# A first weight load moved to another queue and ahead of the other loads, with its conversion two items earlier in the program

## The chip, the cores and the metric

The kernel runs on one core of one Trainium2 chip. The metric is the device time of one execution in microseconds (us), lower is better. The engines are named as the profile names them: PE (TensorE matmul), PEld (its weight load), DVE (VectorE), ACT (ScalarE), POOL (GpSimd) and SP (SyncE, which only issues transfers). "SPq" and "ACTq" are the sequencers of SP and ACT at the moment they issue a transfer.

## What is computed

Three layers follow each other on 3072 tokens (4 batches of 768) of width 512. First comes attention with 8 heads of width 64, in which each query sees 8 global keys and the 96 latest keys, with a distance bias per head. Then a gated layer with float64 weights, and then a "soft" mixture of experts with 32 slots. Cut to what matters:

```
scores = q @ k.T / 8 + bias(head, distance)      # kept where global or local
x  = softmax(scores) @ v                         # 3072 x 512
h  = x @ w_in                                    # w_in 512 x 2048, float64
g  = h * sigmoid(h)
x2 = g @ w_out                                   # w_out 2048 x 512, float64
logits = x2 @ phi                                # 32 slots
slots  = softmax(logits, over tokens).T @ x2
out    = softmax(logits, over slots) @ experts(slots)   # 8 experts: relu(s @ w1) @ w2
```

## The kernel before

**Tiles and stages.** Attention works on 24 tiles `T` of 128 queries, the gated layer on 8 chunks of 3 tiles. Products in the gated layer are made of f16 halves (a high and a low part of each operand), three matmuls for one product. Attention of the first three tiles (T = 0, 1, 2) comes first, alone; after that the matmuls of a chunk are the main line and the attention of the next chunk's tiles is woven in between them.

**Attention of one tile.** `s_step(T, pr)` makes the scores of one pair of heads: two or four matmuls (L316) into the two score banks, on DVE a bias-add with a row minimum for each head (L331, with a small read of the accumulator after it), on ACT the exponential (L332). After two pairs (half a tile) the probabilities are split into a high part (L200 on ACT) and a low part (L208 on DVE) and turned by a transfer (L349, `DMA_TRANSPOSE`, issued by SP). `pv_step` multiplies the turned halves by v (L371). The two score banks are shared by successive pairs, so the matmuls of the next pair start when DVE has read the last one. `load(T)` issues four transfers on SP: q, the two halves of k, and v. `split(T)` makes the two halves of v (L200, L210).

**Float64 weights.** `w_in` and `w_out` arrive as 16 parts of 1024 KB of 64-bit words (L451). `conv(p)` turns part `p` into the two f16 halves with six larger operations that follow each other across the engines: L461 on ACT (takes a byte of each word), L463 on DVE, two short matmuls L468 on PE (a check of bits that must be zero, with the small matrix `wz`), L471 on DVE, then L481 on ACT (high half) and L489 on DVE (low half). `w_ahead()` issues the loads of the next parts whose place is free; parts 1 to 6 are also held back until a given half of an attention tile is done (`GATE`, by a one-column write on POOL, L356). The first matmuls of the gated layer are L503 to L505.

**The prologue** (L779 on) loads the two counts `n_global` and `n_local` and three distance tables (`shapes`, 192 KB) on ACT's queue, and on SP's queue tile 0, the identity matrix (`ident`, 64 KB of `shapes`), tile 1, weight part 0, tile 2 and `phi`. DVE makes the distances from the counts and tables (L794 to L806), then `wz` from `ident` (L811, L812); POOL makes `ident16` from `ident` and then the bias tables of the later tiles (L818); ACT makes the bias table of tile 0 (L814).

**What sets the order.** Program order is written by hand: `first_items()` lists the steps of the first three tiles, and `START` says after which item each of the first parts is converted:

```
START = [3, 9, 14, 18, 22, 99, 99, 99]
...
        for i, it in enumerate(first_items()):
            it()
            while nconv < 8 and before[nconv] <= i:
                conv(nconv)
```

Items 0, 1, 3 and 4 are the four pairs of heads of tile 0, item 2 is the split of tile 1, item 5 its first product with v. From this program a scheduler lays down, at build time, a fixed list for each engine, in which independent steps may change places. Every engine then works through its list in order, and a step that has to wait holds what stands behind it. Transfers use eight counters in turn (`DMAHW0` to `DMAHW7` in the lists), given out in program order: a transfer is not issued before the earlier one on its counter has landed.

Of the kernel before, what the change touches and what calls it, by code (L numbers as in the profile page):

```python
# [10 lines left out]
I32 = mybir.dt.int32  # L11
# [68 lines left out]
        return self.view(self.take(n), dims, dtype)  # L80


START = [3, 9, 14, 18, 22, 99, 99, 99]
AHEAD = [0, 0, 0, 0, 0, 5, 8, 11, 13, 15]
HE = 'AAAAAAAA'
PHE = 'AAAAAAA'
# [14 lines left out]
def fast_kernel(tc, keepp, q_l, k_l, v_l, q_f, k_f, n_global, n_local, w_in, w_out, phi, w1, w2, shapes, pick_c, out):  # L101


    nc = tc.nc
# [5 lines left out]
    with ExitStack() as ctx:  # L110
# [4 lines left out]
        ar = Arena(pool.tile([128, NB // 4], F32, name="arena"), NB)  # L115
# [137 lines left out]
        def paired(T):  # L253

            return T < NPAIR

        def q_of(T):
            return q32[2 if T == 2 else T % 2]

        def load(T, bufs):  # L260
            if paired(T):
                nc.sync.dma_start(out=q_of(T), in_=q_f[T])
                for z in range(2):
                    nc.sync.dma_start(out=kr32[:, z, 0:4, T % NR], in_=k_f[T][:, :, 64 * z:64 * z + 64])
                nc.sync.dma_start(out=v_at[T], in_=v_l[T])
                return
            for s, src in zip(bufs, (q_l, k_l, v_l)):
                nc.sync.dma_start(out=s, in_=src[T])
            staged[T] = bufs
# [26 lines left out]
        def s_step(T, pr):  # L296
# [41 lines left out]
            if lp == 1:  # L338
                pb, ptb = p16[half], pt[half].rearrange("p z h s c -> p (z h s) c")
                if t == 0:  # L340
                    pb = pb.rearrange("p z h c -> p (z h c)")[:, 0:1024].rearrange("p (z h c) -> p z h c", z=2, h=4)
                if T < C0 and PTE[2 * T + half] != "D":
                    n = w // 32
                    flip(ptb[:, 0:n], ptb[:, n:2 * n], pfb.rearrange("p h c -> p (h c)"), PTE[2 * T + half])
                    held = ptb[:, 2 * n - 1, 127:128]
                else:
                    hi(PHE[T] if T < len(PHE) else CFG["phi"], pb[:, 0, :, :w], pfb[:, :, :w], 0)
                    lo(PLE[T] if T < len(PLE) else CFG["plo"], pb[:, 1, :, :w], pfb[:, :, :w], 0, pb[:, 0, :, :w])
                    nc.sync.dma_start_transpose(out=ptb[:, 0:w // 16], in_=pb.rearrange("p z h c -> p (z h c)"))  # L349
                    held = pb[:, 1, 3, w - 1:w]  # L350
                if T < C0:
                    done_p.add((T, half))
                    p = nload[0]
                    if p < 16 and GATE.get(p) == (T, half) and holder.get(place[p]) is None:

                        G.tensor_scalar(out=ar.view(place[p], [16], F32)[:, 0:1], in0=held, scalar1=1.0, scalar2=0.0, op0=ALU.mult, op1=ALU.add)  # L356
                    w_ahead()
# [38 lines left out]
        def first_items():  # L396
            items = []
            for T in range(C0):
                items.append(lambda T=T: s_step(T, 0))
                items.append(lambda T=T: s_step(T, 1))  # L400
                if T:
                    items.append(lambda T=T: pv_step(T - 1, 1))
                if T + 1 < C0:
                    items.append(lambda T=T: split(T + 1))
                else:
                    items.append(lambda T=T: load(C0, stage_m))
                items.append(lambda T=T: s_step(T, 2))
                items.append(lambda T=T: s_step(T, 3))
                items.append(lambda T=T: pv_step(T, 0))
            items.append(lambda: pv_step(C0 - 1, 1))  # L410
            items.append(lambda: split(C0))
            items.append(lambda: load(C0 + 1, stage_m))
            return items
# [27 lines left out]
        place = [wq[0], wq[1], wq[2], wq[3], we[0], we[1], wq[0], wq[1], we[0], wq[2], wq[3], we[1], we[0], wq[3], we[1], we[0]]  # L441
# [2 lines left out]

        done_p = set()

        def w_ahead():
            while nload[0] < most[0] and holder.get(place[nload[0]]) is None and (GATE.get(nload[0]) is None or GATE[nload[0]] in done_p):
                p = nload[0]
                holder[place[p]] = p  # L450
                nc.sync.dma_start(out=ar.view(place[p], [2048], I32), in_=(w_in if p < 8 else w_out)[p % 8].bitcast(I32))  # L451
                nload[0] += 1

        def conv(p):
# [33 lines left out]
            else:  # L488
                V.scalar_tensor_tensor(out=dst[1], in0=src, scalar=-p2(e - 128), in1=dst[0], op0=ALU.mult, op1=ALU.subtract)  # L489
            holder[place[p]] = None  # L490
            w_ahead()


# [286 lines left out]
        for i, src in enumerate((n_global, n_local)):  # L780
            nc.scalar.dma_start(out=cw[:, 2 * i:2 * i + 2], in_=src.bitcast(I32).rearrange("(o n) -> o n", o=1).to_broadcast([128, 2]))
        nc.scalar.dma_start(out=rel.rearrange("p s c -> p (s c)"), in_=shapes[:, 0:384])
        load(0, None)
        nc.sync.dma_start(out=ident, in_=shapes[:, 384:])
        for T in range(1, C0):
            load(T, None)
            if T == 1:
                w_ahead()
        ph = ar.view(g0 + 20480, [4, NS], F32)
        nc.sync.dma_start(out=ph, in_=phi)  # L790
        hi("P", ident16, ident, 0)
# [30 lines left out]
        nconv = 0  # L822
        before = START
        for i, it in enumerate(first_items()):
# [563 lines left out]
```

## Time and profile before

| | |
|---|---|
| time, median of 3 runs | 716.47 us (713.61 to 717.72) |
| the profiled execution's own time | 718.77 us |
| its span, first to last instruction | 717.0 us |
| busy share of the span: PE, DVE, ACT, POOL | 93%, 69%, 51%, 34% |
| mean granted TensorE clock | 0.987 |
| DMA | 120.08 MB, mean 167 GB/s |

The busy shares are means over stages with different limits: the opening with attention alone, the first chunk with the conversion of the weights beside it, a long middle, and the expert layer at the end. So the stages are read one by one, by the busy time of each engine in stretches of the span, and inside the opening by the instructions in order of time and by what ended each wait. A row of the timeline gives start, duration, engine, line, operation, what it writes and reads, how many are merged in it, and in brackets the idle time of its engine just before it with what ended it. DMA shares are means over the core's 16 DMA engines and can pass 1 where transfers overlap in an engine.

### The profile page before, as it was taken

What the parts mean: (1) busy time and instruction counts of PE and PEld (TensorE: products, weight loads), DVE (VectorE), ACT (ScalarE), POOL (GpSimd) and SP (SyncE); (2) the same over time, 40 slices, a digit from 0 to 9 for tenths busy, and PEclk for the clock granted to TensorE, in tenths of its full rate; (3) what the DMA queues carried; (4) which work ended last, traced back from release to release, by engine and by line L of the source; (5) the groups of instructions that cost most, each with busy time, mean ns of one, the idle gap of its engine ahead of it and who ended that gap; (6) DMA issues with size and microseconds to landing.
All of it is one profiled execution on the core that took longest, in us unless ns stands there. A gap on an engine that the chain in (4) does not pass through costs nothing.

```text
span 717.0 us, 13665 instructions
## 1 busy us (share of the span) xinstructions
PE 669.4 (93%) x5175; PEld 387.1 (54%) x5175; DVE 497.6 (69%) x1191; ACT 363.2 (51%) x910; POOL 240.6 (34%) x201
## 2 busy tenths in 40 slices
PE   4779988899999999999999999999999989999992
PEld 2445543356655664566556655665566546665552
DVE  4999889988754876487638763876386159797432
ACT  5678876556523552356235522652265157574322
POOL 3110002125543556254625572346143400280000
PEclk9999999999999999999999999999999999999997
DMA  7999847783572558426734665355433892296998
GB/s 223 236 293 264 263 135 162 221 191 82 114 149 74 114 123 194 93 49 119 163 77 107 141 161 97 81 118 114 65 46 62 224 302 78 80 370 239 388 400 289
DMA packets 165257, 120.08 MB, mean 167 GB/s; under 512 B 143936, under 2 KB 150464, under 8 KB 159168
## 3 DMA queue, kind: packets, MB, share of 16 engines
q1 hardware_dynamic: 163968, 118.15, 62.9%
q10 hardware_dynamic: 1216, 0.99, 0.4%
q8 instruction: 42, 0.69, 0.4%
q14 instruction: 31, 0.25, 0.1%
HBM read 79.01 MB, written 6.29 MB: 119 GB/s over the span
## 4 chain that ended last, share of the span: by engine, by line


## 5 line engine op out<-in xcount | busy, mean ns | idle before, releaser
L202 POOL TENSOR_SCALAR arena<-arena 128x1024 f16<-128x1024 f32 (+4 forms) x107 | 110.2, 1040 | 299.9 <-ACT arena L332 100.5
L503 PE MATMUL bank<-rows,arena 128*128 128x384 f16 x512 | 168.2, 329 | 0.3 <-ACT rows L200 0.3
L504 PE MATMUL bank<-rows,arena 128*128 128x384 f16 x512 | 168.1, 328 | 0.0
L505 PE MATMUL bank<-rows,arena 128*128 128x384 f16 x512 | 168.0, 328 | 0.0
L200 ACT ACTIVATE arena<-bank 128x384 f16<-128x384 f32 (+1 forms) x153 | 77.3, 505 | 149.9 <-DVE bank L509 85.8
L332 ACT ACTIVATE arena<-arena 128x256 f32<-128x256 f32 (+1 forms) x192 | 92.4, 482 | 84.8 <-DVE arena L331 83.6
L524 PE MATMUL bank<-arena 128*128 128x512 f16 x336 | 127.7, 380 | 1.1 <-DVE arena L489 1.0
L525 PE MATMUL bank<-arena 128*128 128x512 f16 x336 | 127.6, 380 | 0.0
L523 PE MATMUL bank<-arena 128*128 128x512 f16 x336 | 126.6, 381 | 0.7 <-ACT arena L481 0.7
L210 DVE SCALAR_TENSOR_TENSOR arena<-bank,arena 128x384 f16<-128x384 f32 (+2 forms) x154 | 87.7, 570 | 29.5 <-ACT arena L200 28.7
L208 POOL TENSOR_TENSOR arena<-arena 128x1024 f16<-128x1024 f32 (+1 forms) x43 | 89.4, 2080 | 25.4 <-ACT arena L200 22.5
L331 DVE CUSTOM_DVE_ANT_0 arena<-bank,arena 128x256 f32<-128x256 f32 (+1 forms) x192 | 70.2, 394 | 30.9 <-PE bank L326 27.7
L509 DVE SCALAR_TENSOR_TENSOR bank<-arena,bank 128x384 f32<-128x384 f32 x128 | 71.2, 558 | 29.2 <-ACT arena L507 28.2
L208 DVE TENSOR_TENSOR arena<-arena 128x1024 f16<-128x1024 f32 (+2 forms) x52 | 69.4, 1334 | 9.9 <-POOL arena L202 8.8
L200 ACT ACTIVATE arena<-arena 128x1024 f16<-128x1024 f32 (+1 forms) x69 | 62.0, 904 | 19.6 <-DVE arena L210 8.4
L210 DVE SCALAR_TENSOR_TENSOR arena<-arena 128x1024 f16<-128x1024 f32 (+3 forms) x64 | 64.2, 1017 | 7.3 <-POOL arena L202 4.2
L505 PEld LDWEIGHTS <-arena 128*128 128x128 f16 x512 | 50.4, 98 | 33.8 <-issue 1.0
L503 PEld LDWEIGHTS <-arena 128*128 128x128 f16 x512 | 50.5, 99 | 33.2 <-issue 5.0
L507 ACT ACTIVATE arena<-bank 128x384 f32<-128x384 f32 x128 | 61.6, 481 | 12.3 <-PE bank L505 11.5
L504 PEld LDWEIGHTS <-arena 128*128 128x128 f16 x512 | 50.4, 98 | 28.3 <-issue 1.0
L525 PEld LDWEIGHTS <-arena 128*128 128x128 f16 x336 | 33.0, 98 | 41.9 <-issue 3.6
L523 PEld LDWEIGHTS <-arena 128*128 128x128 f16 x336 | 32.8, 98 | 36.2 <-issue 2.6
(185 smaller groups left out, 814.5 us busy)
## 6 DMA issues: line engine op xcount, KB each, us to landing
arena<-in_w_dram SPq DMA_DIRECT2D x31, 1024.0 KB, 8.5
arena<-in_q_l_dram SPq DMA_DIRECT2D x18, 512.0 KB, 3.7
arena<-in_k_l_dram SPq DMA_DIRECT2D x18, 512.0 KB, 4.3
arena<-in_w_in_dram SPq DMA_DIRECT2D x8, 1024.0 KB, 6.0
arena<-in_w_out_dram SPq DMA_DIRECT2D x8, 1024.0 KB, 6.0
arena<-in_v_l_dram SPq DMA_DIRECT2D x24, 256.0 KB, 3.3
out_dram<-arena SPq DMA_DIRECT2D x4, 768.0 KB, 8.6
arena<-in_q_f_dram SPq DMA_DIRECT2D x6, 256.0 KB, 5.2
```

The costliest lines, as they stand in the source:

```text
L200: A.activation(out=out, in_=in_, func=AF.Copy, scale=p2(e))
L202: G.tensor_scalar(out=out, in0=in_, scalar1=p2(e), scalar2=0.0, op0=ALU.mult, op1=ALU.add)
L208: (V if eng == "V" else G).tensor_tensor(out=out, in0=in_, in1=h, op=ALU.subtract)
L210: return V.scalar_tensor_tensor(out=out, in0=in_, scalar=p2(e), in1=h, op0=ALU.mult, op1=ALU.subtract)
L332: A.activation(out=pw, in_=pw, func=AF.Exp, scale=-1.0, bias=nmx[:, T, h:h + 1], accum_out=psum_[T % 2][:, h:h + 1])
L503: mm(hp, wh, x[:, 0, k], start=(k == 0), stop=False)
L504: mm(hp, wh, x[:, 1, k], start=False, stop=False)
L505: mm(hp, wl, x[:, 0, k], start=False, stop=(k == 3))
L509: gated.append(V.scalar_tensor_tensor(out=hp, in0=th, scalar=1.0, in1=hp, op0=ALU.add, op1=ALU.mult))
L523: mm(op, gh, woh[:, f, 0], start=(f == 0), stop=False)
L524: mm(op, gh, woh[:, f, 1], start=False, stop=False)
L525: mm(op, gl, woh[:, f, 0], start=False, stop=(f == 15))
```

## The change

Weight part 0 is no longer loaded by SP after tile 1, but by ACT's queue, right behind the tables and ahead of everything that SP loads in program order; and its conversion is written after item 1 instead of after item 3.

```diff
-START = [3, 9, 14, 18, 22, 99, 99, 99]
+START = [1, 9, 14, 18, 22, 99, 99, 99]
...
-        def w_ahead():
+        def w_ahead(queue=nc.sync):
...
-                nc.sync.dma_start(out=ar.view(place[p], [2048], I32), in_=(w_in if p < 8 else w_out)[p % 8].bitcast(I32))
+                queue.dma_start(out=ar.view(place[p], [2048], I32), in_=(w_in if p < 8 else w_out)[p % 8].bitcast(I32))
...
         nc.scalar.dma_start(out=rel.rearrange("p s c -> p (s c)"), in_=shapes[:, 0:384])
+        w_ahead(nc.scalar)
         load(0, None)
         nc.sync.dma_start(out=ident, in_=shapes[:, 384:])
         for T in range(1, C0):
             load(T, None)
-            if T == 1:
-                w_ahead()
```

The lists of the engines change from the start to about the 300th row of DVE's list, and not behind that. Three places follow. The first is ACT's list, from the load of the tables on (L814 is L813 in the changed file). Before:

```order
L782 DMA arena<-in_shapes_dram 128x384
L814 ACT_TABLE_LOAD
L814 ACTIVATE arena<-arena 128x128 x8
L200 ACTIVATE arena<-arena 128x8x64
L332 ACTIVATE arena<-arena 128x128 x4
L200 ACTIVATE arena<-arena 128x8x64
L200 ACTIVATE arena<-arena 128x512
L332 ACTIVATE arena<-arena 128x128 x3
L461 ACTIVATE arena<-arena 128x1024
```

And with the change:

```order
L782 DMA arena<-in_shapes_dram 128x384
L451 DMA arena<-in_w_in_dram 128x2048
L813 ACT_TABLE_LOAD
L813 ACTIVATE arena<-arena 128x128 x8
L200 ACTIVATE arena<-arena 128x8x64
L332 ACTIVATE arena<-arena 128x128 x4
L461 ACTIVATE arena<-arena 128x1024
L200 ACTIVATE arena<-arena 128x512
L200 ACTIVATE arena<-arena 128x8x64
```

The load of part 0 stands ahead of the table load, and the first step of its conversion (L461) ahead of the split of tile 0's first half (L200, 128x512), where it stood behind that split and behind seven of tile 0's eight exponentials (L332).

The second is DVE's list at the end of tile 0's scores (128x128; tile 1's are 128x256). Before:

```order
L331 ISA arena<-bank_70,arena 128x256
L331 ISA arena 128x1
L463 TENSOR_SCALAR arena<-arena 128x1024
L331 ISA arena<-bank_71,arena 128x256
L331 ISA arena 128x1
L382 TENSOR_SCALAR arena<-arena 128x8
L471 SCALAR_TENSOR_TENSOR arena<-arena 128x1024
L208 TENSOR_TENSOR arena<-arena 128x512
```

And with the change:

```order
L331 ISA arena<-bank_71,arena 128x128
L331 ISA arena 128x1
L463 TENSOR_SCALAR arena<-arena 128x1024
L208 TENSOR_TENSOR arena<-arena 128x512
L471 SCALAR_TENSOR_TENSOR arena<-arena 128x1024
L210 SCALAR_TENSOR_TENSOR arena<-arena 128x4x32
L210 SCALAR_TENSOR_TENSOR arena<-arena 128x8x64
L331 ISA arena<-bank_70,arena 128x256
```

L463 and L471 have moved from between and behind the second pair of tile 1 to straight behind tile 0's last pair; the L208 that the first turning transfer waits for now stands behind L463.

The third is SP's list, with what each transfer waits for, from the load of `ident` on. Before:

```order
L784 DMA arena<-in_shapes_dram 128x128
L262 DMA arena<-in_q_f_dram 128x512 [waits DMAHW0_49]
L264 DMA arena<-in_k_f_dram 128x4x64 [waits DMAHW1_49]
L264 DMA arena<-in_k_f_dram 128x4x64 [waits DMAHW2_49]
L265 DMA arena<-in_v_l_dram 128x512 [waits DMAHW3_49]
L451 DMA arena<-in_w_in_dram 128x2048 [waits DMAHW4_49]
L262 DMA arena<-in_q_f_dram 128x512 [waits DMAHW5_49]
```

And with the change, from the load of `ident` and then from the load of `phi`:

```order
L785 DMA arena<-in_shapes_dram 128x128 [waits DMAHW0_49]
L262 DMA arena<-in_q_f_dram 128x512 [waits DMAHW1_49]
L264 DMA arena<-in_k_f_dram 128x4x64 [waits DMAHW2_49]
...
L789 DMA arena<-in_phi_dram 128x128 [waits DMAHW1_49]
L264 DMA arena<-in_k_f_dram 128x4x64 [waits DMAHW2_49]
L264 DMA arena<-in_k_f_dram 128x4x64 [waits DMAHW3_49]
L265 DMA arena<-in_v_l_dram 128x512 [waits DMAHW4_49]
L349 DMA_TRANSPOSE arena<-arena 128x8x128 [waits DMAHW5_49,DVE_49,Pool_49]
```

Part 0 has taken a counter, so all later transfers are one counter further on: `ident` now waits for counter 0, which `n_global` uses. And the loads of k and v of tile 3 stand ahead of the first turning transfer; before, they stood some ten places behind it.

## Rows read from the trace of the kernel before

**Rows 1.** Busy time by stage: us, then each engine's busy time, clock, DMA

```profile
9.40:52.60 43.20, 31.92 (x198) 19.32 (x198) 38.72 (x95) 33.35 (x81) 9.14 (x17) 1.00 0.96 260
52.60:170.00 117.40, 108.61 (x728) 56.81 (x728) 106.41 (x212) 83.49 (x187) 15.33 (x12) 0.97 0.74 198
170.00:570.00 400.00, 399.06 (x3143) 235.31 (x3142) 259.65 (x695) 175.34 (x522) 189.60 (x142) 1.00 0.53 110
```

**Rows 2.** What DVE waited for in 9 to 53 us: total, times, longest

```profile
DVE arena L331 <- PE bank L316: 2.0, 3, 1.1
DVE arena L208 <- ACT arena L200: 0.8, 2, 0.5
DVE arena L331 <- ACT arena L332: 0.8, 1, 0.8
DVE arena L471 <- PE bank L468: 0.6, 2, 0.4
```

**Rows 3.** Timeline of the first 10 us: start, duration, engine, instruction

```profile
1.65 0.45 ACTq L782 DMA_DIRECT2D arena<-in_shapes_dram  x1
...
3.24 0.43 SPq L784 DMA_DIRECT2D arena<-in_shapes_dram  x1
4.36 0.33 SPq L262 DMA_DIRECT2D arena<-in_q_f_dram  x1
...
7.04 0.43 SPq L451 DMA_DIRECT2D arena<-in_w_in_dram  x1
...
8.13 0.30 POOL L202 TENSOR_SCALAR arena<-arena 128x128 f16<-128x128 f32 x1 [1.18 <-DMA arena<-in_shapes_dram]
...
8.82 0.33 DVE L811 SCALAR_TENSOR_TENSOR arena<-arena 128x32 f32<-128x32 f32 x2
...
9.49 0.28 DVE L331 CUSTOM_DVE_ANT_0 arena<-bank,arena 128x128 f32<-128x128 f32 x1
```

**Rows 4.** Transfers issued before 20 us: queue, count, KB each, median us to landing

```profile
arena<-in_shapes_dram SPq DMA_DIRECT2D x1, 64.0 KB, 4.8
```

**Rows 5.** Busy time by stretch, columns as in rows 1; last two: DMA share, GB/s

```profile
0.00:6.00 6.00, 0.00 (x0) 0.00 (x0) 0.48 (x5) 1.28 (x1) 0.82 (x9) 1.00 0.40 110
6.00:9.00 3.00, 0.80 (x4) 0.54 (x4) 2.18 (x11) 0.40 (x2) 0.53 (x3) 1.00 1.17 319
9.00:12.50 3.50, 2.08 (x9) 1.50 (x9) 1.90 (x16) 3.50 (x17) 3.36 (x7) 1.00 1.04 391
```

**Rows 6.** DMA queues in 4.5 to 6 us: packets, MB, share (q1 SP's, q10 ACT's)

```profile
q1 hardware_dynamic: 712, 0.19, 54.7%
q10 hardware_dynamic: 209, 0.20, 37.3%
```

**Rows 7.** Timeline of 12 to 21 us, part 0's conversion and tile 1's scores

```profile
12.27 1.13 ACT L200 ACTIVATE arena<-arena 128x512 f16<-128x512 f32 x2
...
15.37 1.36 SPq L349 DMA_TRANSPOSE arena<-arena  x1
...
17.31 0.42 DVE L331 CUSTOM_DVE_ANT_0 arena<-bank,arena 128x256 f32<-128x256 f32 x1 [1.07 <-PE bank L316]
...
17.66 1.30 DVE L463 TENSOR_SCALAR arena<-arena 128x1024 uint16<-128x1024 uint16 x1
...
19.67 1.23 DVE L471 SCALAR_TENSOR_TENSOR arena<-arena 128x1024 int32<-128x1024 int32 x1 [0.38 <-PE bank L468]
...
20.71 0.82 PE L371 MATMUL bank<-arena 128*128 128x64 f16 x12
```

**Rows 8.** DVE's groups in 9.4 to 24.8 us: count | busy us, mean ns

```profile
L210 DVE SCALAR_TENSOR_TENSOR arena<-arena 128x512 f16<-128x512 f32 x3 | 2.1, 687 | 0.0
...
L208 DVE TENSOR_TENSOR arena<-arena 128x512 f16<-128x512 f32 x2 | 1.4, 678 | 0.0
...
L489 DVE SCALAR_TENSOR_TENSOR arena<-arena 128x1024 f16<-128x1024 f32 x1 | 1.2, 1221 | 0.0
```

**Rows 9.** What ACT waited for in 10 to 60 us

```profile
ACT arena L461 <- DMA arena<-in_w_in_dram: 4.0, 2, 2.6
```

## The prediction

> **What bounds the kernel now.** I read the busy time by stage first, because one mean over the span hides where a gain can count. From 170 to 570 us PE is busy 399.06 of 400 us [rows 1]: there nothing can be won or lost by loads and conversions, and whatever the opening gains or loses is handed on unchanged to the end. In the opening it is another engine: from the first score step to the first matmul of the gated layer (9.4 to 52.6 us) DVE is busy 38.72 of 43.2 us and PE only 31.92 [rows 1]. So the question is what the change does to DVE's list up to about 52 us. The work on it is the same; only its waits can change. What DVE waited for in that stretch is 2.0 + 0.8 + 0.8 + 0.6 = 4.2 us in all [rows 2], and that is the most that any filling of gaps can bring there, 0.6% of the time. The third view is the timeline of the first 21 us with the transfers [rows 3 to 7], to see which of these waits the change touches and which new one it can make.
>
> **The change part by part.** Sums are made against the profiled execution, 718.77 us (span 717.0 and 1.77 around it); the median of the runs is 716.47, 2.3 lower, and the forecast is put on the median.
>
> *Issue on ACT, one transfer fewer on SP.* An issue on ACT's sequencer takes 0.45 us [rows 3]. It delays the load of ACT's table, but ACT's work of the first 6 us is that load alone, 1.28 us [rows 5], and 0.45 more still ends inside them; its next work waits for DVE's tables: cost nothing. SP's 0.43 us at 7.04 [rows 3] goes; SP's next loads then wait for counters or for full DMA engines: gain nothing.
>
> *Where the megabyte moves.* Part 0 was issued at 7.04 [rows 3]; it will be issued near 2.1, behind the tables (issue at 1.65, 0.45 long). It does not start at once: ACT's queue is still moving the tables in 4.5 to 6 us, 209 packets and 0.20 MB, next to SP's queue [rows 6]. So I expect its bytes from about 6 us on, not in the idle DMA time before (share 0.40 over the first 6 us, rows 5). From 6 us to past 12 the DMA engines are full, share 1.17 and 1.04 [rows 5], so what part 0 gains there, SP's loads lose. The rate of a stretch with its 1.05 MB in it is 391 GB/s [rows 5]: 2.7 us of all engines. Alone, part 0 would be through at 8.7, at half speed at 11.4; ACT's L461 comes to it behind the first four exponentials, in the place where two L200 start at 12.27 now [rows 7]: no wait taken.
>
> *Who loses: `ident`.* DVE's L811 needs `ident`, and stands in front of the first L331. Before, `ident` was issued at 3.24 and landed 4.8 us later [rows 3, 4], at 8.04: POOL started on it at 8.13 and DVE at 8.82 [rows 3], 0.8 us to spare. Now two things push it. Its issue waits for counter 0, that is for `n_global` to land; the q load that waited for that counter before was issued at 4.36 [rows 3], so that is 1.1 us later than 3.24. And its bytes, behind tile 0's v in SP's queue, share the engines with part 0. Lower end: SP's queue is behind anyway, the later issue costs nothing and small packets pass: landing 8.04, no delay. Upper end: all of part 0 first and the later issue in full: 8.04 + 2.7 + 1.1 = 11.84, 3.0 us after 8.82. In 4.5 to 6 us the two queues shared the engines, 54.7% to 37.3% [rows 6], neither shut out; with such a sharing about half of part 0's 2.7 us falls before `ident`, 1.3, and of the 1.1 about half: landing near 9.9, and the first L331 moves from 9.49 to about 10.5. **+1.0 us** (0 to +3.0). POOL's `ident16` moves as much, and its bias tables with it; they are used by tile 1 only, and tile 1's first L331 moves back too: nothing.
>
> The Trainium skill's page "DMA: Bandwidth & Descriptors", section "Queues, rings and completion order", says that each DMA engine goes round its queues packet by packet; rows 6 agree that neither queue is shut out. By that rule part 0 gets every second turn against all of SP's loads, and as its rows (8 KB for each partition) are longer than theirs (2 KB and less), most of the time until it is through; the start term would lie near +2 and the sum at +0.9.
>
> *Conversion sooner.* L463 runs at 17.66 now, between two pairs of tile 1, and L471 at 19.67 behind a wait of 0.38 for PE's L468 [rows 7]. The L331 before L463 waited 1.07 us for the scores of tile 1's second pair [rows 7], since nothing else stood between two pairs that share the score banks. With the change L463, L208, L471 and two L210 come before tile 1's first pair, and L489 and L208 between its first and second: 1.2 + 0.7 us of work [rows 8] where DVE waited 1.07. That wait goes: **-1.1 us**. The wait for L468 stays, because only one L208 (0.7 us, rows 8) stands between L463 and L471: 0. Bounds: 0, if the wait only moves to tile 1's third pair, and -2.0, if all three waits of L331 for PE go [rows 2].
>
> *First turning transfer later.* L208 of tile 0's first half now stands behind L463 (1.30 us) but ahead of one L210 (0.7, rows 8): 0.6 us later, with the start 1.6. The transfer went out at 15.37 and its first user, L371, ran at 20.71 [rows 7], landing to use over 2 us: covered, 0. Without that cover it would cost up to 1.6 on PE, not on DVE.
>
> *Tile 3's k and v before it.* These 512 KB move at 391 GB/s [rows 5] in 1.3 us. SP issues them when tile 1's loads have landed, which PE needs before tile 1's scores and so before the L208 in question: no hold for the turning transfer, whose cover of 2 us takes in the 1.3 too. Later they are missing from the stretch in which L461 waited 4.0 us for its loads [rows 9], a wait of ACT and not of DVE. 0 (-1.3, if such a wait reaches DVE, to +1.3, if they hold the first turning transfer beyond its cover).
>
> *The new order up to 165 us.* Same instructions, other neighbours. From 52.6 to 170 us DVE is idle 11.0 us and PE 8.8 [rows 1]; I have no row that says which way these go. 0, bounds 2 us either way.
>
> **Sum:** +1.0 - 1.1 + 0 = -0.1 us, so 718.7 for the profiled execution and **716.4 us** on the median. A measurement of this kernel tells some 0.5% from no change, 3.6 us; the forecast is no measurable change, between 714 and 719.
>
> **Rivals.**
> *Slower: `ident` behind the megabyte.* The upper end above: DVE stands at L811 until 11.84, +3.0, and as tile 1's loads come as late, the wait of 1.07 is not filled but moves; with the 0.38 in front of L471 doubled the sum is +3.4, 719.9. It decides at a landing of 8.82 us: each us beyond is one of DVE. For it: full DMA engines and the 0.8 us to spare. Against it: the two queues shared in rows 6, and SP's queue is busy with v in any case. The round-robin rule of the Trainium skill cited above speaks for it. Chance 0.16, about half of it past 0.5%.
> *Faster: gaps closed everywhere.* Part 0 is converted while tile 0's data are still on the way, `ident` is not late, and with L463 to L489 out of tile 1 and the early loads of tile 3 the rest of the list meets ready data: the 4.2 us of rows 2 go, 712.3. For it: the loads for which L461 waited 4.0 us [rows 9]. Against it: in the new list L463 comes only after tile 0's last L331, so the waits before 14 us stay. Chance 0.20.
> *Not what it says.* If ACT's queue is served last, part 0 comes behind all that moves from 6 to 12.5 us: 3.0 x 1.17 + 3.5 x 1.04 = 7.2 us of full engines [rows 5], until 13.2. Then `ident` is on time, but L461 holds ACT, and through it L463 holds DVE, by 13.2 - 12.3 = 0.9 us. The start term is as large as before, and the case lies inside the forecast.
>
> **How the numbers follow.** Forecast 0.64, slower rival 0.16, faster rival 0.20. Faster by over 0.5%: 0.15 of the faster rival and 0.04 of the forecast's order term, 0.19. Slower by over 0.5%: 0.07 of the slower rival and 0.05, 0.12. Within: 0.69. The range reaches to both rivals' times, 712.6 to 720.0, and leaves out about 0.2.
>
> **What would show it.** In the changed profile: the first packets of ACT's queue beyond the tables near 6 us; L811 at 9 to 11 us and the first L331 0.7 after it; L463 near 15 us with no L331 waiting 1.07 for PE behind it; the first L503 within 1.5 us of 52.6; PE as full from 170 to 570 us. The prediction is wrong if L811 waits past 11.8, if L463 waits for the load, if L371 begins to wait over 2 us for the turning transfers, or if the stretch from 52.6 to 170 us changes its length by more than 2 us.

## The result and the profile after

The changed kernel takes 722.06 us (median of 6 runs, 719.53 to 725.01), the kernel before on the same chip 715.64 us (6 runs): ratio 1.0092, 95% interval 1.0062 to 1.0121. Run once more among the experiments, it took 722.81 us against 716.95, ratio 1.0083 [1.0057, 1.0108]. The change costs about 6 us, nearly twice the 0.5% that a measurement of this kernel can tell, and the time lies beyond both ranges that the prediction gives (714 to 719, and 712.6 to 720.0 further down). The profiled execution of the change took 725.01 us (span 723.2), 6.2 more than that of the kernel before, so the two traces show a difference of the measured size.

Two places make it up. The first is the start. The first timeline rows answer to [rows 3]; the load of `ident` is L785 here and L784 there, and behind that loop line numbers are one lower than before (L810 here is L811 there). Timeline of the change, first 13 us:

```profile
2.13 0.47 ACTq L451 DMA_DIRECT2D arena<-in_w_in_dram  x1
...
4.43 0.33 SPq L785 DMA_DIRECT2D arena<-in_shapes_dram  x1
...
10.99 0.80 PE L316 MATMUL bank<-arena 64*128 64x128 f32 x4 [10.99 <-DMA arena<-in_k_f_dram]
...
11.79 0.44 DVE L810 SCALAR_TENSOR_TENSOR arena<-arena 128x32 f32<-128x32 f32 x2 [2.01 <-DMA arena<-in_shapes_dram]
11.84 0.33 POOL L202 TENSOR_SCALAR arena<-arena 128x128 f16<-128x128 f32 x1 [3.80 <-DMA arena<-in_shapes_dram]
...
12.71 0.28 DVE L331 CUSTOM_DVE_ANT_0 arena<-bank,arena 128x128 f32<-128x128 f32 x1
```

Part 0 goes out on ACT's queue at 2.13. `ident` goes out at 4.43 instead of 3.24 and DVE stands 2.01 us at L810 for it, until 11.79 instead of 8.82 [rows 3]. The first L331 starts at 12.71 instead of 9.49: 3.2 us lost. Its landing, in the view of transfers issued in 4.5 to 6 us (as [rows 4]):

```profile
arena<-in_shapes_dram SPq DMA_DIRECT2D x1, 64.0 KB, 7.3
```

7.3 us instead of 4.8. The queues show why. In 7 to 9 us of the change (q1 is SP's queue, q10 ACT's: packets, MB, share of the 16 engines):

```profile
q10 hardware_dynamic: 98, 0.77, 94.2%
q1 hardware_dynamic: 137, 0.05, 9.4%
```

and in the same 2 us of the kernel before:

```profile
q1 hardware_dynamic: 1269, 0.62, 117.2%
```

SP's queue, with all of the tiles' loads on it, falls from 1269 packets to 137 while part 0 moves. Neither queue is shut out by count (137 packets to 98), but a packet of part 0 is 0.77 MB / 98 = 7.9 KB and one of SP's 0.4 KB, so SP gets 6% of the bytes. Being first in did not help either: tile 0's k was issued at 1.21 us, ahead of part 0 at 2.13, and PE's first L316 waited for it until 10.99.

The second place is at 158 to 168 us. Three rows of the change, one an engine, from their timelines:

```profile
161.60 1.62 POOL L202 TENSOR_SCALAR arena<-arena 128x1024 f16<-128x1024 f32 x2 [14.51 <-DMA arena<-in_k_l_dram]
...
162.67 1.62 DVE L208 TENSOR_TENSOR arena<-arena 128x1024 f16<-128x1024 f32 x1 [3.20 <-POOL arena L202]
...
167.84 0.38 PE L545 MATMUL bank<-arena 128*128 128x64 f16 x8 [2.79 <-DVE arena L548]
```

Read from the top: POOL waits for a k load, DVE 3.20 us for POOL, PE 2.79 us for DVE. In the kernel before this is PE's longest wait from 145 to 170 us:

```profile
PE bank L524 <- DVE arena L489: 0.3, 1, 0.3
```

The load is tile 9's k, and SP's queue tells why it is late. Timeline of SP's queue of the change (L536 is the turning transfer of chunk 0's second product):

```profile
150.67 0.33 SPq L268 DMA_DIRECT2D arena<-in_q_l_dram  x1
152.00 1.24 SPq L536 DMA_TRANSPOSE arena<-arena  x1
153.28 1.32 SPq L349 DMA_TRANSPOSE arena<-arena  x1
154.69 2.98 SPq L536 DMA_TRANSPOSE arena<-arena  x2
157.72 0.57 SPq L268 DMA_DIRECT2D arena<-in_k_l_dram  x1
```

and of the kernel before:

```profile
145.34 0.33 SPq L268 DMA_DIRECT2D arena<-in_k_l_dram  x1
147.07 0.33 SPq L268 DMA_DIRECT2D arena<-in_v_l_dram  x1
149.12 2.62 SPq L536 DMA_TRANSPOSE arena<-arena  x2
```

DVE's L208 on tile 8's k, which frees the place that tile 9's k is loaded into, before and in the change:

```profile
144.10 1.21 DVE L208 TENSOR_TENSOR arena<-arena 128x1024 f16<-128x1024 f32 x1
```

```profile
152.08 1.22 DVE L208 TENSOR_TENSOR arena<-arena 128x1024 f16<-128x1024 f32 x1
```

Before, k goes out at 145.34, when that L208 is done. In the change DVE takes tile 7's first scores first, that L208 comes at 152.08, and three L536 stand ahead of k on SP: 157.72, 12.4 us later. Of these, 8.0 us are the later end of L208 (153.30 instead of 145.31), and the other 4.4 the transfers that still stand ahead of k then. Nothing of this touches the line that was edited; it is the new order of lists, 150 us downstream.

The stages, answering to [rows 1] (us, then busy time of PE, PEld, DVE, ACT, POOL, clock, DMA share, GB/s):

```profile
9.40:52.60 43.20, 31.08 (x164) 17.94 (x165) 35.09 (x90) 31.83 (x81) 9.23 (x18) 1.00 0.97 251
52.60:170.00 117.40, 106.80 (x721) 55.54 (x719) 107.71 (x210) 81.41 (x177) 14.49 (x11) 0.97 0.70 196
170.00:570.00 400.00, 399.29 (x3147) 236.04 (x3145) 262.43 (x701) 178.29 (x532) 188.27 (x141) 1.00 0.53 109
```

PE is as full from 170 us on as before, so what the opening lost is handed on: the tanh of block 28 runs at 181.83 us before and at 186.79 in the change, block 60 at 329.85 and 334.88. Below, "late by" is this difference against the profiled kernel before, at the tanh (L507) of a block counted through all chunks; in the change it is +7.5 us at block 0, +2.2 at block 18, +5.5 at block 20, and +5.0 from block 28 to block 76. In the repeated run it is +5.7, +0.8, +4.0 and +5.1.

The profiled kernel before has a loss of its own, which shifts these figures. From block 12 (93.16 us) to block 13 it takes 4.68 us, the change 2.89, and two experiments below whose lists there are those of the kernel before (`extra_megabyte`, `swap_alone`) 3.20. The stage of 90 to 100 us, before and in the change (the clock is the third figure from the end):

```profile
90.00:100.00 10.00, 8.07 (x56) 4.33 (x57) 8.91 (x22) 8.39 (x18) 0.00 (x0) 0.83 0.43 82
```

```profile
90.00:100.00 10.00, 9.23 (x91) 5.38 (x89) 10.00 (x26) 9.83 (x23) 1.99 (x1) 1.00 0.43 82
```

In the kernel before PE was busy for 0.07 us of 90 to 92 us, and in 94 to 96 us its granted clock was 0.50, the lower of its two levels (1.2 GHz): an L503 took 0.53 us there and 0.33 once the clock was back. `swap_and_megabyte` has such a stretch at the same place, the other runs have the full clock there, and of these `extra_megabyte` and `swap_alone` idle as long before it, so why the clock fell stays open. Against a kernel before without it, "late by" would be about 1.5 us more from block 13 on: 6.4 in the change from block 28 on, which is the measured difference.

### The profile page after: what moved, and what is told of

Its sections match the earlier page's. It is cut to its first block, busy times and chain, and to the rows that moved or that the text cites. A ratio compares the mean times of both kernels' runs of the same rounds, so it can differ in the third digit from the quotient of the medians.

```text
span 723.2 us, 13665 instructions
## 1 busy us (share of the span) xinstructions
PE 672.1 (93%) x5175; PEld 387.6 (54%) x5175; DVE 498.3 (69%) x1191; ACT 362.9 (50%) x910; POOL 235.9 (33%) x201
## 4 chain that ended last, share of the span: by engine, by line
## 5 line engine op out<-in xcount | busy, mean ns | idle before, releaser
L503 PE MATMUL bank<-rows,arena 128*128 128x384 f16 x512 | 167.7, 328 | 0.7 <-ACT rows L200 0.7
L200 ACT ACTIVATE arena<-bank 128x384 f16<-128x384 f32 (+1 forms) x153 | 77.1, 504 | 155.0 <-DVE bank L509 91.1
L332 ACT ACTIVATE arena<-arena 128x256 f32<-128x256 f32 (+1 forms) x192 | 92.3, 483 | 82.1 <-DVE arena L331 81.1
L210 DVE SCALAR_TENSOR_TENSOR arena<-bank,arena 128x384 f16<-128x384 f32 (+2 forms) x154 | 87.7, 570 | 29.1 <-ACT arena L200 28.4
L208 POOL TENSOR_TENSOR arena<-arena 128x1024 f16<-128x1024 f32 (+1 forms) x43 | 89.4, 2079 | 26.1 <-ACT arena L200 23.3
L331 DVE CUSTOM_DVE_ANT_0 arena<-bank,arena 128x256 f32<-128x256 f32 (+1 forms) x192 | 70.2, 395 | 29.9 <-PE bank L326 27.8
L208 DVE TENSOR_TENSOR arena<-arena 128x1024 f16<-128x1024 f32 (+2 forms) x52 | 69.5, 1336 | 12.7 <-POOL arena L202 12.0
L200 ACT ACTIVATE arena<-arena 128x1024 f16<-128x1024 f32 (+1 forms) x69 | 62.2, 906 | 16.8 <-DVE arena L210 8.3
L210 DVE SCALAR_TENSOR_TENSOR arena<-arena 128x1024 f16<-128x1024 f32 (+2 forms) x64 | 64.2, 1018 | 7.1 <-POOL arena L202 4.3
L507 ACT ACTIVATE arena<-bank 128x384 f32<-128x384 f32 x128 | 61.6, 481 | 13.5 <-PE bank L505 12.7
L503 PEld LDWEIGHTS <-arena 128*128 128x128 f16 x512 | 50.4, 98 | 33.0 <-issue 4.9
```

Of the source, the lines that this page charges most:

```text
L200: A.activation(out=out, in_=in_, func=AF.Copy, scale=p2(e))
L208: (V if eng == "V" else G).tensor_tensor(out=out, in0=in_, in1=h, op=ALU.subtract)
L210: return V.scalar_tensor_tensor(out=out, in0=in_, scalar=p2(e), in1=h, op0=ALU.mult, op1=ALU.subtract)
L332: A.activation(out=pw, in_=pw, func=AF.Exp, scale=-1.0, bias=nmx[:, T, h:h + 1], accum_out=psum_[T % 2][:, h:h + 1])
L503: mm(hp, wh, x[:, 0, k], start=(k == 0), stop=False)
```

## The experiments

The first theory: two separate costs, the starved loads at the start and tile 9's k at 158 to 168 us. Rivals: all of it comes from the start; or all of it from conversion placed ahead of tile 1. Single profiles of one kernel can differ by 1.8 us at a mark (the change: block 0 late by 7.5, its repeat by 5.7); the ratios with their intervals carry the verdicts, the marks say where.

### The megabyte alone (`extra_megabyte`)

Kernel before, with one more load that nobody reads, on ACT's queue; every engine's list stays as it was, but for some 15 neighbouring instructions of PE.

```diff
         nc.scalar.dma_start(out=rel..., in_=shapes[:, 0:384])
+        nc.scalar.dma_start(out=ar.view(g0, [2048], I32), in_=w_in[0].bitcast(I32))
         load(0, None)
```

> The kernel before with one more load of 1024 KB on ACT's queue, behind the tables, into memory that nothing reads; every engine's list is that of the kernel before apart from this load. Theory A (the early megabyte starves SP's loads, and the lost start is handed on): ident late as in the changed kernel, first L331 at about 12.7 us instead of 9.49, L503 3 us later, time +3 us (718.5 to 719.5). Theory B (the start is made up later, the new order of the lists costs the 6.4 us): first L331 late, but time within 1 us of before. Theory C (all of the 6.4 us is the lost start and what follows from it): +6 us.

Measured: 719.24 us, ratio 1.0044 [1.0028, 1.0060], +3.2 us. DVE's timeline:

```profile
11.61 0.44 DVE L811 SCALAR_TENSOR_TENSOR arena<-arena 128x32 f32<-128x32 f32 x2 [1.92 <-DMA arena<-in_shapes_dram]
...
12.55 0.28 DVE L331 CUSTOM_DVE_ANT_0 arena<-bank,arena 128x128 f32<-128x128 f32 x1
```

Late by 3.1 us at every mark up to block 12 and by 1.7 from block 28 on, which is 3.2 with the 1.5 us of the kernel before; no jump at 158 us (PE's longest wait for L548 there is 0.3). So the second queue's megabyte alone makes the loss of the start, and about half of the change's cost. It is a megabyte more than the change moves, but `queue_only` below, which moves none more, has its first L331 nearly as late (12.21).

### `ident` ahead of tile 0 on SP (`ident_first`)

```diff
-        load(0, None)
         nc.sync.dma_start(out=ident, in_=shapes[:, 384:])
+        load(0, None)
```

> The changed kernel with the load of ident moved to the front of SP's queue, lists otherwise as in the changed kernel. Theory A: ident lands near 4 to 6 us and no longer holds DVE, but the second half of tile 0's k is still behind part 0 (10.99 us in the changed kernel), so the first L331 comes at about 11.8 instead of 12.7, time 1 us under the changed kernel (721). If ident alone were the hold, the first L331 would come at 9.5 and the time fall by 3.2 us.

Measured, on the changed kernel: 721.23 us, ratio 1.0084 [1.0063, 1.0105]; nothing gained. DVE's timeline:

```profile
12.66 0.29 DVE L331 CUSTOM_DVE_ANT_0 arena<-bank,arena 128x128 f32<-128x128 f32 x1 [2.82 <-PE bank L316]
```

`ident` no longer holds DVE; PE does, whose first L316 waits for tile 0's k until 11.74. Theory A had 11.8 for the first L331. Tile 0's k is late as `ident` was: what is put first only says which load is waited for.

### Part 0 held back behind the tables' first use (`tied_to_bias`, `tied_at_three`)

Part 0 stays on ACT's queue, but is issued behind the first L814, at 8.6 us (8.5 in the other run); `tied_at_three` also puts its conversion back behind the third item.

```diff
-        w_ahead(nc.scalar)
         load(0, None)
...
             near = A.activation(out=bias0[:, h], ...)
+            if h == 0:
+                with tc.issue_after(near.ins):
+                    w_ahead(nc.scalar)
```

```diff
-START = [1, 9, 14, 18, 22, 99, 99, 99]
+START = [3, 9, 14, 18, 22, 99, 99, 99]
```

> The changed kernel with part 0's load on ACT's queue tied behind the first bias table (L814), so it is issued near 8.7 us, when tile 0's data and ident have landed. Theory A: first L331 at 9.5 as before, and the time goes back to that of before or under it (714 to 717). Theory B: the lists are still new (conversion ahead of tile 1's scores), so 2 to 3 us over before remain (718 to 719), with a first L503 later than 53.5 us.

> The changed kernel with part 0's load on ScalarE's queue held behind ScalarE's first L814, as in the run tied_to_bias, and its conversion left where the kernel before has it, behind the third item. From about 100 us on all lists are those of the kernel before, tile 9's k load ahead of the turning transfers included. Theory (the change loses at the start by the second queue's megabyte and at 160 us by tile 9's k load, and by nothing else that lasts): the first L331 starts at 9.5 to 9.8 us, tile 1's scores up to 2 us late because the megabyte now runs beside tile 1's and 2's loads, no jump at 160 us, from 170 us on within 1.5 us of the kernel before, and the time within 2 us of it. Rival (the queue as such costs, wherever the megabyte runs, since it holds SP's loads back for 3 us in any place): the stretch from 170 us on 3 us late, the time 719 to 720. Rival on the other side (SP's queue without a megabyte ahead of tile 2 is a gain): 1 us or more sooner than the kernel before from 170 us on.

Measured: 723.63 us, ratio 1.0129 [1.0095, 1.0163], and 721.37 us, 1.0081 [1.0056, 1.0105]. In both the first L331 is on time (9.63 and 9.47), and both are slow all the same. `tied_at_three`, three engines' rows:

```profile
17.22 0.30 POOL L202 TENSOR_SCALAR arena<-arena 128x128 f16<-128x128 f32 x1 [4.09 <-DMA arena<-in_phi_dram]
17.55 0.29 DVE L210 SCALAR_TENSOR_TENSOR arena<-arena 128x128 f16<-128x128 f32 x1 [2.78 <-POOL arena L202]
...
19.87 1.56 PE L316 MATMUL bank<-arena 64*128 64x256 f32 x4 [4.15 <-DVE arena L331]
```

The megabyte now starves the next loads: `phi` lands late, DVE's list has `phi`'s L210 ahead of tile 1's scores, and the kernel is 3.9 us late at tile 1 (its first L331 at 19.39 instead of 15.46). POOL starts on `phi` at 17.22 here and at 15.88 before, so 1.3 of DVE's 2.78 us is the later landing, and the rest the place of that L210 in the new list. There is no jump at 158 us, since from about 100 us on the lists are those of the kernel before. My theory for `tied_at_three` (within 2 us of before) fell. The first rival, that the queue as such costs wherever the megabyte runs in the opening, comes nearer, but it had 3 us (719 to 720) and the run is 5.8 us above the kernel before; what the queue and what the new list have of that is not separated here. That `tied_to_bias` costs 3 us more (1.6 by the marks) fits the jump, which it has (PE waits 2.7 us for L548).

### The queue without the earlier conversion (`queue_only`)

The change with `START = [3, ...]` as before.

> The changed kernel with START back at 3. Theory A: first L331 at 12.7 as in the changed kernel, time that of the changed kernel within 2 us. Theory B (the order of the lists is what costs): the lists differ again, so the time moves by 2 us or more to one side while the first L331 stays at 12.7.

Measured: 719.87 us, ratio 1.0052 [1.0028, 1.0076]; first L331 at 12.21, jump at 158 us present (2.6 us). Beginning the conversion sooner is no gain on top of the queue. By the medians it is 2 to 3 us worse, but the intervals overlap and the marks do not repeat it (late by 5.7 from block 28 on here, by 5.0 and 5.1 in the change), so a loss isn't shown either. The other half, `START` alone with part 0 on SP, leaves all lists as in the kernel before, and so wasn't run.

### Tile 8 split first (`tile8_first`, `ident_and_tile8`, `queue_and_tile8`)

The change, `ident_first` and `queue_only`, each with DVE's split of tile 8 ahead of tile 7's first scores, as before the change. The lists up to 140 us are those of the kernel that each is based on.

```diff
+                if T == 7:
+                    items.append(lambda: split(8))
+                    items.append(lambda: load(9, stage_m))
-                items.append(lambda T=T: s_step(T, 0))
+                items.append(lambda T=T: behind(T, 0))
...
+        def behind(T, pr):
+            with tc.issue_after(last_lo[0].ins) if T == 7 else ExitStack():
+                s_step(T, pr)
```

> The changed kernel with one thing put back as the kernel before has it: VectorE splits tile 8 ahead of tile 7's first scores, so that tile 9's k load stands ahead of the turning transfers at L536 on SP's queue. All lists up to 140 us are those of the change. Theory (the rearranged order costs its 3 us at one place: tile 9's k is issued at 157.7 us instead of 145.3, GpSimd's L202 waits for it until 161.6, VectorE's L208 waits 3.2 us for GpSimd and TensorE 2.8 us for VectorE): the jump between the tanh of block 18 (156 to 158 us) and block 20 (161 to 166 us) goes from +3.3 to about 0, the stretch from 170 us on is late by about 2 us instead of 5.0, and the time falls by about 3 us against the change, to about 719. Rival (TensorE is short of work there for another reason, such as the block of scores that was moved): the wait comes back behind another instruction, the stretch stays late by about 5 us and the time stays at 722.

> The same as the run tile8_first, with the load of ident put first on SP's queue as in the run ident_first. Theory (two costs, at the start and at tile 9's k, that add up, and the rest of the new order gives back what the start lost): ident_first was at -0.5 us at block 18 and at +2.8 at block 20, so without the jump it is level with the kernel before from 170 us on, within 1 us, and the time is about 716 to 718. Rival (the new order loses its 3 us wherever it can): late by 2.3 us from 170 us on as ident_first, the time 719 to 721.

> The run queue_only (part 0 on ScalarE's queue at once, its conversion behind the third item) with VectorE's split of tile 8 put ahead of tile 7's first scores, as in the run tile8_first. Theory: the jump of about 3 us at 158 to 168 us goes (from +1.5 at block 18 and +5.7 behind 170 us in queue_only to +1.5 to +3 behind 170 us), and the time falls from 1.0052 of the kernel before to about 1.001 to 1.003. Rival: the stall comes back elsewhere and the ratio stays at 1.005.

> The changed kernel once more, beside the others on one chip. If the lists alone set the time, the first L331 starts at 12.7 us, the stretch from 170 to 470 us is late by 5.0 us within 0.3, and the time is 722 within 1. If the 5.0 us was an accident of the one profiled execution, it moves by more than 1 us.

| pair | without, ratio | with, ratio |
|---|---|---|
| the change (repeated beside it) | 1.0083 [1.0057, 1.0108] | 1.0049 [1.0029, 1.0068] |
| `ident_first` | 1.0084 [1.0063, 1.0105] | 1.0038 [1.0018, 1.0059] |
| `queue_only` | 1.0052 [1.0028, 1.0076] | 1.0054 [1.0033, 1.0075] |

The mean of the three differences is 0.26%, 1.9 us; two pairs show 2.4 and 3.3, the third nothing; in the first and the third the intervals overlap. The marks have nearly the same mean in other pairs: from block 28 on the pairs are late by 5.0 and 4.3, 2.3 and 2.8, 5.7 and 0.1, so one profiled execution does not settle a pair. They agree on the place: from block 18 to 28 the lateness grows by 2.8 (4.3 in the repeat), 2.8 and 4.2 us without the edit and shrinks by 0.5 to 0.6 with it. Counted from block 14, since the new order gains 1.0 to 2.1 just before the jump, it grows by 1.4 (3.0), 0.7 and 3.2 without, and by 0.7, -0.9 and 0.1 with it. In the traces k goes out sooner, though not as soon as before: SP's queue of `tile8_first`

```profile
152.57 0.57 SPq L269 DMA_DIRECT2D arena<-in_k_l_dram  x1
153.53 4.95 SPq L544 DMA_TRANSPOSE arena<-arena  x3
```

and its PE waits in 155 to 170 us

```profile
PE bank L553 <- DVE arena L556: 1.2, 1, 1.2
```

against 2.8 in the change and 0.8 to 1.2 in all three. So the wait shrinks by less than the theory said, and `ident_and_tile8` did not come level with the kernel before as I had expected: 2.7 us are left. The time of the third pair stays unexplained: its profiled execution, 716.0 us, is the fastest of its ten and is level with the kernel before from block 28 on, but its median is not.

### An order like it put into the kernel before (`swap_alone`, `swap_and_megabyte`)

Kernel before; tile 8 is split behind tile 7's first scores, so that tile 9's k falls behind the turning transfers. Start and opening untouched; the second run adds the extra megabyte.

```diff
+        def behind(T):
+            with tc.issue_after(last_red[0].ins) if T == 7 else ExitStack():
+                split(T + 1)
...
-                    items.append(lambda T=T: split(T + 1))
+                    items.append(lambda T=T: behind(T))
```

> The kernel before with one order of the change forced on it: VectorE splits tile 8 behind tile 7's first scores, so that the load of tile 9's k stands behind the three turning transfers at L536 on SP's queue. All lists up to 140 us, the whole start included, are those of the kernel before, and from about 190 us on as well. Theory (this order is worth about 3 us of the change's 6): nothing moves before 150 us, a wait of VectorE's L208 for GpSimd's L202 and one of TensorE for VectorE appear between 155 and 170 us, the stretch from 170 us on is late by 2 to 4 us, and the time is 1.003 to 1.005 of the kernel before. Rival (the wait in the change's trace only took up slack that the late start had left): within 1 us of the kernel before, ratio below 1.002.

> The run swap_alone with the extra megabyte of the run extra_megabyte on ScalarE's queue at the start: the two suspected costs of the change together, and nothing else of it (part 0 and its conversion stay as in the kernel before). Theory (the two costs add up and are the whole of the change): the first L331 at 12.5 us, late by 5 to 7 us behind 170 us, and the time 1.007 to 1.010 of the kernel before, as the change. Rival (the lateness of the start lets the loads catch up, so the second cost is hidden by the first): as extra_megabyte alone, 1.003 to 1.005.

Measured: 722.04 us, ratio 1.0084 [1.0060, 1.0109], and 723.08 us, 1.0099 [1.0075, 1.0123]. SP's queue of `swap_alone`:

```profile
147.17 4.01 SPq L541 DMA_TRANSPOSE arena<-arena  x3
152.96 1.23 SPq L350 DMA_TRANSPOSE arena<-arena  x1
160.25 0.33 SPq L269 DMA_DIRECT2D arena<-in_q_l_dram  x1
164.21 1.87 SPq L350 DMA_TRANSPOSE arena<-arena  x1
166.18 1.00 SPq L269 DMA_DIRECT2D arena<-in_k_l_dram  x1
```

and DVE's L208 on tile 8's k and on tile 9's:

```profile
160.96 1.24 DVE L208 TENSOR_TENSOR arena<-arena 128x1024 f16<-128x1024 f32 x1
...
171.85 1.62 DVE L208 TENSOR_TENSOR arena<-arena 128x1024 f16<-128x1024 f32 x1 [2.21 <-POOL arena L202]
```

This order alone costs 6 us in a kernel whose start is untouched, twice the 3 that the theory gave it. It goes further than the change's: L208 on tile 8's k ends at 162.20 instead of 153.30, one more L350 stands ahead of k, and k goes out at 166.18, 8.5 us later than in the change. By the marks it takes 4.1 us (from 1.9 early at block 20 to 2.2 late at block 36), and 4.1 again on top of the megabyte (1.6 to 5.7). By the ratios the two together are 1.0099, more than either and less than the sum (1.0128), though with intervals of 0.5% that does not show that one covers part of the other, and by the marks none is covered.

### Smaller rows on the second queue (`small_rows`)

`extra_megabyte` with the place in SBUF laid out with gaps, to make its rows as short as the tiles' ones.

```diff
-    ...(out=ar.view(g0, [2048], I32), in_=w_in[0].bitcast(I32))
+    ...(out=ar.view(g0, [32, 128], I32)[:, :, 0:64], in_=w_in[0]... in rows of 64)
```

> The kernel before with the same extra megabyte on ScalarE's queue as in the run extra_megabyte, but laid down in rows of 256 bytes (in the extra load the place in SBUF has gaps, the bytes are the same). Only the first 12 us are read: the lists differ behind the first scores. Theory (the 16 engines take the two queues' rows in turn, one for one, so a row of 8192 bytes holds a row of 256 back for its whole time): with equal rows SP's queue has about half of the bytes in 7 to 9 us instead of 0.06 of 0.81 MB, and the first L331 starts 0.5 to 1.5 us later than in the kernel before instead of 3.1. Rival (the megabyte goes first whatever its rows are, since its queue got its requests in first): the first L331 at 12.5 us again or later. Second rival (it is the total of bytes that counts, shared evenly): as the theory at 7 to 9 us, but the first L331 still 2 us or more late.

The theory's numbers did not come, and the time of the first rival did (12.5 us or later): DVE stands at L811 until 14.19 and the first L331 starts at 15.12, 5.6 us late; the one time is 723.03 us. The queues in 7 to 9 us, here and in `extra_megabyte`:

```profile
q10 hardware_dynamic: 117, 0.44, 98.9%
q1 hardware_dynamic: 214, 0.05, 11.8%
```

```profile
q10 hardware_dynamic: 95, 0.76, 93.7%
q1 hardware_dynamic: 226, 0.06, 12.7%
```

The packets did not get as short as meant: 0.44 MB / 117 = 3.8 KB each, holding an engine 0.989 x 16 x 2 / 117 = 0.27 us, while those of `extra_megabyte` are of 8 KB and held it for 0.32 us each. So a packet of half the size took nearly the same time, the megabyte took longer, and SP's queue was starved for longer. Whether equal packets would share fairly stays open. What was issued ahead of the megabyte fared otherwise than what was issued behind it: tile 0's k landed sooner than in `extra_megabyte`, where PE's first L316 waited for it until 10.96,

```profile
8.54 0.80 PE L316 MATMUL bank<-arena 64*128 64x128 f32 x4 [8.54 <-DMA arena<-in_k_f_dram]
```

and `ident`, issued behind it, later. That is as the first rival has it (the queue that got its requests in first goes first), so this rival is not excluded for short packets; with long ones it fails, since k is late there too.

None of these versions is faster than the kernel before; those with the megabyte on the second queue all lie at a ratio of 1.0038 or more.

## Why the prediction was wrong

**What bounds the kernel**: right. PE is full behind 170 us (399.29 of 400) and hands the loss on.

**Issue on ACT, and where the megabyte moves**: right. ACT's table load is 0.5 us later and nobody waits for it; part 0's bytes move from 6 us on and are through near 9.5.

**Who loses: `ident`**: right in the mechanism, mis-sized, and this is the first failed step: the share of the engines that was left to SP's queue. It took +1.0 of a bound of 0 to +3.0; measured +3.2. The upper end put the landing at 11.84; DVE started at 11.79. The fault was the row it was weighed by: in [rows 6] the two queues shared the engines 54.7% to 37.3%, but there both moved short packets (0.20 MB / 209 = 1 KB on ACT's queue, 0.3 KB on SP's). With packets of 8 KB on ACT's queue SP's was left 6% of the bytes. The slower rival had nearly this price (+3.0), and was given 0.16; its time, 719.9, is short of 722.06 too, since it does not have the second place. The round-robin rule of the Trainium skill ("DMA: Bandwidth & Descriptors", section "Queues, rings and completion order") speaks of turns by packet, and the trace agrees so far that neither queue is shut out by count: 137 packets to 98, though that is not one to one. The +2 that I had worked out from it was still short of the 3.2. `extra_megabyte` (+3.2 us) shows that this term alone is about half of the loss.

**Conversion sooner, -1.1**: a failed step too: the wait went and the gain did not come. The row "L331 <- PE L316: 2.0, 3 times" of [rows 2] is gone from DVE's waits in 9 to 53 us; the longest there now are

```profile
DVE arena L208 <- ACT arena L200: 2.0, 1, 2.0
DVE arena L810 <- DMA arena<-in_shapes_dram: 2.0, 1, 2.0
DVE arena L331 <- ACT arena L332: 1.6, 2, 0.8
DVE arena L489 <- ACT arena L481: 0.7, 1, 0.7
```

and the timeline of the change that answers to [rows 7]:

```profile
17.23 1.29 DVE L463 TENSOR_SCALAR arena<-arena 128x1024 uint16<-128x1024 uint16 x1
...
19.11 1.36 SPq L349 DMA_TRANSPOSE arena<-arena  x1
...
21.45 0.42 DVE L331 CUSTOM_DVE_ANT_0 arena<-bank,arena 128x256 f32<-128x256 f32 x1
```

L463 is only 0.43 us earlier, since the start was late, and tile 1's scores wait behind the conversion: their first L331 at 21.45 instead of 15.46, and block 0 is 7.5 us late (5.7 in the repeat). By block 18 that is 2.2 (0.8), but the lists do the same work in another order by then, so these marks do not tell what this step alone brings. No run shows a gain from it: `queue_only`, without it, is no slower.

**First turning transfer later, tile 3's loads before it**: right at 0. The transfer went out 3.7 us later (19.11), and L371 waits less for its transfers, 1.0 us in 9 to 60 us instead of 3.8.

**The new order up to 165 us, 0 within 2 us**: a failed step as well. It lost 1.4 to 3.0 us between blocks 14 and 28, at one place: tile 9's k, 12.4 us late because DVE frees its place 8.0 us later and because turning transfers stand ahead of it on SP. That such an order is the cause is shown by putting a like one into the kernel before (+6 us, with k later still) and by taking it out of the change and of `ident_first` (-2.4 and -3.3 us); in `queue_only` taking it out gave nothing in the time, though the jump went, so its size in the change, 1.4 to 3 us, is less sure than its cause. The prediction said that it had no row on this and put the middle of its bounds. Such rows could be had: which loads the new lists have behind L536 and behind DVE's scores, and in SP's rows before, what each of these transfers takes.

The sum by the marks, with 1.5 us added behind block 12 for the kernel before: +3.2 at the first L331, +0.4 from there to block 18, +2.8 from block 18 to block 28, 6.4 us, as between the medians (722.06 - 715.64). In the repeated run, whose first L331 starts at 12.24, it is +2.8, -0.4 and +4.3, 6.6 us against 5.9. The total holds; what each part has of it is known to some 1.5 us. Of the signs that the prediction named, L810 came at 11.79, just under the 11.8, while the first L503 came at 57.8 instead of within 1.5 us of 52.6.

## What to carry to other kernels

A second DMA queue is not spare bandwidth: before a large load is put on it, look up in the trace which small loads of the other queue are on the path in that stretch, and price them as if the large one went first. When an edit lets a scheduler rearrange the lists, look in the new lists, however far from the edit, for every load that has moved behind a transfer which waits for something else, and for every step that frees a load's place and has moved back; each is a term of its own. Before marks of two single profiles are compared, compare their granted clocks: here 1.5 us of the difference was the reference's own. A stage that loses 3 us because of a load will not get them back from a stage that is full.

## What the runs showed of the hardware

With two queues at work, both got packets through, 1.4 to 2.4 of SP's to one of ACT's in 7 to 9 us (137 to 98 in the change, 226 to 95 in `extra_megabyte`; 712 to 209 in [rows 6], where both were short). The bytes went with the packets' size: SP's queue fell from 0.62 to 0.05 MB in 2 us. That the engines take the queues in turn is the reading that fits these counts; none of these runs shows it by itself. And in one profiled execution of `small_rows` a packet with half the bytes, laid down with gaps, held its engine nearly as long (0.27 us to 0.32) as a whole one, so that the 16 engines moved 248 GB/s in place of 406 in that stretch at a full share.
